# Fewer TensorE products ahead of the first MLP layer: Newton on -F and -E, paired landmarks, and batch 0's later A scores moved beside batch 1's

## The chip, the core and the metric

The kernel runs on one core of one Trainium2 chip. A core has TensorE (PE; its weight loads are listed apart as PEld), VectorE (DVE), ScalarE (ACT), GpSimd (POOL), SyncE (SP) and 16 DMA engines. Each engine works through its own list of instructions in order, and semaphores make one wait for another. The time is the device time of one execution in microseconds (us); lower is better. The kernel before took 277.86 us, the median of three runs (276.68 to 277.95).

## What is computed

Nyström attention over 8 batches of 8 heads (576 tokens, head size 64), then a two-layer MLP (512 to 2048 to 512, SiLU between) over its 4608 token rows:

```
q_lm = q.reshape(B, H, 32, 18, 64).mean(axis=3)      # 32 landmarks
k_lm = k.reshape(B, H, 32, 18, 64).mean(axis=3)
A  = softmax(q    @ k_lm^T / 8)     # 576 x 32
Bm = softmax(q_lm @ k_lm^T / 8)     # 32 x 32
C  = softmax(q_lm @ k^T    / 8)     # 32 x 576
Z  = Bm^T / (norm1(Bm) * norminf(Bm) + 1e-6)
repeat 6 times: Z = 2*Z - Z @ Bm @ Z
x  = A @ Z @ C @ v                  # heads side by side: 4608 x 512
out = silu(x @ w_in) @ w_out        # silu(h) = h * sigmoid(h)
```

## The kernel before

The eight batches go through the core one after another. For each batch there is an attention part, which makes two small things: AT, the normalised A scores transposed (line 630), and mb (lines 646 and 666), which is Z C v folded into w_in, so that the first layer is one product of mb and AT. The layer loop (line 831 on) runs 16 steps s for each batch b. A step makes 256 rows of the hidden layer (l1, line 680), runs SiLU on ACT (line 700), and adds products of the second layer of earlier tokens (l2_mm, 708; cnt says how many). The attention part of batch b+1 is woven into the steps of batch b, so that TensorE has both. The order is written out by hand: what stands in the code is the order of each engine's list.

Only batch 0 has no layers to be woven into; its attention part is the straight stretch of lines 738 to 826. Fillers (idle, line 120: products of zeros that no one reads) keep TensorE busy between its steps. DMA loads are issued by POOL, from lines 115 to 144 and from load_w_in and load_w_out calls within the stretch; POOL does some arithmetic too, in the same list.

One batch's attention part goes like this, in the names of the code. The numbers after j are the pieces of q and k: 1 and 0 are k and q of heads 0 to 3, 3 and 2 those of heads 4 to 7.

- transpose_qk (182): q and k transposed on DVE, 32x32 blocks.
- landmarks_pe (189): the sum over the 18 tokens of a landmark, as 18 products with the identity; landmarks_out (196) scales it on ACT; lm_t (254) transposes it on DVE; bd_expand (260) lays it out block-diagonally for the A scores.
- b_scores, b_max, b_exp, b_norm (268 to 315): Bm.
- c_scores, c_max, c_exp (417 to 446): C, with a transpose on TensorE and a copy (c_transpose, c_out); w_mm (476) multiplies by v, w_out (487) scales to W.
- a_scores(i), a_max(i), a_shift(i), a_exp(i), a_norm(i) for three parts i of the 576 tokens (538 to 608): A. a_shift takes the maximum off by a product on TensorE; a_norm is a_sum and a_rec on DVE and a_mul on POOL. a_transpose and a_out (611 to 630) make AT.
- z_mm, z_out, m_unit(f) or m_pair(f): mb, in four quarters f.

Between b_norm and z_mm stands the Newton iteration, in the coordinates F = Bm^T Bm / c and E = Bm / c (c is the product of the norms). Each round makes new F and E by one product with F. For batches 0 and 1 ("tiled") the state that is held is I - F, beside -E: the square of I - F is the new I - F, so for that half a copy out of PSUM is the whole step, but the E half needs E added, which ns_mm (366) does by eight more products with the identity:

```
365	
366	        def ns_mm(self, last=False):
...
379	            if self.tiled:
380	                for g in range(2):
381	                    for h in range(4):
382	                        p = slice(32 * h, 32 * h + 32)
383	                        mm(self.p[p, g, w:], ident[p, p], self.fx[p, g, w:],
384	                           start=False, stop=True)
```

ns_step (386) is the copy, on DVE or ACT by the call. Each mm() (line 77) is a weight load and a matmul on TensorE.

PSUM has eight banks, in four pools: psh (two buffers of two banks: c scores, c transposes of batch 0, atp, hps), pso (two banks: idle, batch 0's later A scores, mp, ops), psn (one: lmp, bb) and psa (one: batch 0's first A scores, wp, mp). A buffer's next user waits until the last reader of the one before is done. In before, some fillers of batch 0 write into the spare half of the c-transpose buffer (spare_bank, 228).

Of the kernel before, what the change touches and what calls it, by code (L numbers as in the profile page):

```python
# [9 lines left out]
BF = mybir.dt.bfloat16  # L10
AF = mybir.ActivationFunctionType
OP = mybir.AluOpType
AX = mybir.AxisListType


# [26 lines left out]
def kernel(  # L42
# [131 lines left out]
    nc.vector.tensor_copy(out=ident, in_=ident_f)  # L174

    eye = constp.tile([128, L], BF, tag="eye", name="eye")
    with nc.allow_low_precision(reason="zeros and ones"):
        nc.vector.tensor_reduce(out=eye, in_=ident_f.rearrange("p (h l) -> p l h", l=L),
                                op=OP.add, axis=AX.X)

# [44 lines left out]
    SPLIT = [256] + [HF] * (B - 1)  # L225
    zeros_in = []

    def spare_bank(x):
        zeros_in[:] = [x[:, 1, :]]
        return x  # L230

    class Att:
# [122 lines left out]
        def f_out(self):  # L355
            w = self.fw
            self.p = self.bb[:, 0:2 * (w + L)].rearrange("p (g n) -> p g n", g=2)
            if self.tiled:
                for g in range(2):
                    nc.vector.scalar_tensor_tensor(  # L360
                        out=self.fx[:, g, 0:w], in0=self.f0[:, g, :], scalar=self.nrm[:, g:g + 1],
                        in1=eye, op0=OP.mult, op1=OP.add)
                return
            nc.vector.tensor_tensor(out=self.fx[:, :, 0:w], in0=self.f0,  # L364
                                    in1=self.nrm.unsqueeze(2).to_broadcast((128, 2, w)),
                                    op=OP.mult)

        def ns_mm(self, last=False):
            w = self.fw
            lo = w if last else 0  # L370
            for g in range(2):
                if self.tiled:
                    for h in range(4):
                        p = slice(32 * h, 32 * h + 32)
                        mm(self.p[p, g, lo:], self.fx[p, g, 0:w], self.fx[p, g, lo:],
                           start=(g == 0), stop=False)
                else:
                    mm(self.p[:, g, lo:], self.fx[:, g, 0:w], self.fx[:, g, lo:],
                       start=(g == 0), stop=True)
            if self.tiled:  # L380
                for g in range(2):
                    for h in range(4):
                        p = slice(32 * h, 32 * h + 32)
                        mm(self.p[p, g, w:], ident[p, p], self.fx[p, g, w:],
                           start=False, stop=True)

        def ns_step(self, copy=nc.vector.tensor_copy):
            w = self.fw
            n = nsp.tile([128, 2, w + L], BF, tag=f"fx{w}", name="fx", bufs=3)
            if self.tiled:  # L390
                copy(out=n, in_=self.p)  # L391
            else:
                nc.vector.scalar_tensor_tensor(  # L393
                    out=n, in0=self.fx, scalar=2.0, in1=self.p, op0=OP.mult, op1=OP.subtract)
            self.fx = n


        def x_out(self):
            w = self.fw
            if self.tiled:  # L400
                self.x = nsp.tile([128, 2, L], BF, tag="x", name="x")
                nc.vector.tensor_scalar(out=self.x, in0=self.p[:, :, w:], scalar1=-1.0,
                                        scalar2=None, op0=OP.mult)
                return
# [47 lines left out]
        def c_transpose(self, g):  # L452
            if not self.by_dma:
                self.t[g] = (pso1("ctp", BF) if self.b else
                             spare_bank(ps2("ctp"))[:, 0, :].bitcast(BF))
# [20 lines left out]
        def w_mm(self):  # L476
            vv = self.v.rearrange("p h (c d) -> p h c d", d=Dh)
            self.w = psa1("wp")[:, 0:2 * Dh].rearrange("p (g d) -> p g d", d=Dh)
            for g in range(2):
# [7 lines left out]
        def w_out(self):  # L487
            self.W = attp.tile([128, 2, Dh], BF, tag="W", name="W", bufs=1)
            for g in range(2):
                if g == 0 and self.b == 0:  # L490
                    nc.vector.tensor_scalar(out=self.W[:, g, :], in0=self.w[:, g, :],
                                            scalar1=self.wsc[:, g:g + 1], scalar2=None,
                                            op0=OP.mult)
                    continue
                nc.scalar.activation(out=self.W[:, g, :], in_=self.w[:, g, :], func=AF.Copy,
# [21 lines left out]
        def z_out(self):  # L517
            self.zwT = attp.tile([128, 4, L], BF, tag="zwT", name="zwT")
            if self.tiled:
                for k, copy in enumerate((nc.vector.tensor_copy, nc.scalar.copy)):  # L520
                    copy(out=self.zwT[:, k::2, :],
                         in_=self.zt[k].rearrange("p (g l) -> p g l", l=L))
            else:
# [108 lines left out]

        def m_unit(self, f, *copy, parts=1):
            self.m_done = f + 1
# [8 lines left out]
            for c0 in range(0, 512, 512 // parts):  # L643
                for r in range(2):
                    c = slice(c0, c0 + 512 // parts)
# [92 lines left out]
    wt = pso1("idle")  # L738
    idle(wt, 9, 512)
    lp = psn1("lmp")  # L740
    landmarks_pe(0, lp, 1, 1)
    transpose_qk(0, 1)
    landmarks_out(0, lp, 1, 1)
    idle(wt, 8)
    landmarks_pe(0, lp, 0, 1)
    transpose_qk(0, 0)
    landmarks_out(0, lp, 0, 1)
    idle(wt, 10)
    a = Att(0)
# [4 lines left out]
    landmarks_out(0, lp, 3, 1)  # L754
    idle(wt, 4)
    landmarks_pe(0, lp, 2, 1)
    transpose_qk(0, 2)
    landmarks_out(0, lp, 2, 1)
    idle(wt, 11)
    a.lm_t(1)  # L760
# [7 lines left out]
    a.a_scores(0)  # L768
    a.a_scores(2)
    a.a_scores(1)  # L770
    a.c_max(0)
# [5 lines left out]
    a.c_transpose(0)  # L777
    idle(zeros_in[0], 8)
    a.c_out(0, nc.scalar.copy)
    a.ns_mm()  # L780
    a.c_max(1)
    idle(zeros_in[0], 4)
    a.ns_step(nc.scalar.copy)
    a.c_exp(1)
    a.ns_mm()
    a.ns_step()
    a.a_max(0)
    idle(zeros_in[0], 4)
    a.ns_mm()
    a.ns_step(nc.scalar.copy)  # L790
    a.c_transpose(1)
    a.ns_mm()
    a.c_out(1, nc.scalar.copy)
    a.a_shift(0)
    a.a_exp(0)
    a.ns_step()
    a.w_scale()
    a.a_max(1)
    load_w_out(0)
    load_w_out(1)  # L800
# [24 lines left out]
    landmarks_pe(1, lp0[:, 0, :], 0, 1, (9, 18))  # L825
    landmarks_out(1, lp0[:, 0, :], 0, 2)

# [3 lines left out]
    for b in range(B):  # L831
# [14 lines left out]
        for s in range(NDC):  # L846
# [3 lines left out]
            if s <= d and b < 2:  # L850
                l1(s)
                act(s)
                if s == 0:
                    lp = psn1("lmp")
                if b == 1:
                    landmarks_pe(2, lp, ORD[s], 1)
# [40 lines left out]
            elif s == d + 2:  # L897
                n = cnt[s]
                a.a_start()
                a.a_scores(0)  # L900
                a.a_scores(1)
                a.c_max(1)
                a.a_max(0)
                a.a_max(1)
                a.c_exp(0)
                a.c_exp(1)
                if b:
                    l2_mm(min(n - 4, 6))
# [175 lines left out]
```

## Time and profile before

| what | us |
|---|---|
| median of three runs | 277.86 |
| the profiled execution, whole | 278.91 |
| its span, first to last instruction | 277.2 |
| TensorE busy, matmuls | 259.0 (93%) |
| ACT busy | 178.2 (64%) |
| DVE busy | 151.9 (55%) |
| POOL busy | 117.7 (42%) |
| TensorE busy in the first 60 us | 49.64 |
| first product of layer 1 starts | 27.14 |
| first SiLU starts | 28.18 |
| f_mm of batch 1 (start of its Newton iteration) | 40.88 |

Times in the profile count from the first instruction. A line of the timeline has start, duration, engine, line, operation and shape, and in brackets the engine's idle time before it and what ended that. "issue" is idle time for which the profile shows no cause. The page's 40 slices are 6.93 us each; a digit is a tenth. PEclk is the clock granted to TensorE, of full speed; in the window view it is the first number behind the engines' columns. DMA share is the mean busy share of the 16 DMA engines, and may go over 1.00 where transfers overlap.

Where the batch-0 stretch and the first layer steps stand: k and q of batch 0 land at 5.54, 6.96, 9.10 and 10.48 us; w_mm runs from 19.82 to 23.19; the layer loop starts at 27.14; batch 1's scores start at 33.91, and its exponentials need the Exp table on ACT (34.63 to 36.12) and then the Silu table again (41.48 to 42.98).

### The profile page before, as it was taken

How to read it: one execution, taken by the hardware profiler on the slowest of the kernel's cores; microseconds unless marked ns; L12 is line 12 of the kernel's file. 1: busy time of each engine (PE TensorE's matmuls, PEld its weight loads, DVE VectorE, ACT ScalarE, POOL GpSimd, SP SyncE). 2: the span in 40 equal slices, each digit the busy share in tenths (PEclk: the TensorE clock that was granted, in tenths of full speed). 3: DMA queues.
4: the chain of work that ended last, by engine and by line, in shares of the span. 5: the costliest groups of instructions: out<-in, count | busy, mean ns of one | idle time of the engine just before them, and what ended most of it. 6: DMA issues, size and time to landing. Idle time of an engine off the chain costs nothing.

```text
span 277.2 us, 7127 instructions
## 1 busy us (share of the span) xinstructions
PE 259.0 (93%) x2920; PEld 149.8 (54%) x2958; DVE 151.9 (55%) x379; ACT 178.2 (64%) x341; POOL 117.7 (42%) x169
## 2 busy tenths in 40 slices
PE   7876879999999999999999999999999999999994
PEld 3654645557565456555655555455645565555541
DVE  5764578264769565838684856836784653100000
ACT  2354686686946985669766965788578846646511
POOL 8434044611598439751895179333971030100000
PEclk9997779999999999999999999999999999999999
DMA  6999999392888791919656955605091312110111
GB/s 107 194 211 207 206 206 169 72 201 65 144 175 135 136 190 48 156 43 197 106 77 133 191 135 78 145 38 97 14 187 47 95 50 71 40 76 38 40 76 76
DMA packets 37792, 32.38 MB, mean 117 GB/s; under 512 B 18816, under 2 KB 29056, under 8 KB 37760
## 3 DMA queue, kind: packets, MB, share of 16 engines
q0 software_dynamic: 15104, 18.35, 41.2%
q1 hardware_dynamic: 22656, 13.57, 18.8%
q8 instruction: 23, 0.38, 0.5%
q14 instruction: 9, 0.07, 0.1%
HBM read 36.70 MB, written 9.44 MB: 166 GB/s over the span
## 4 chain that ended last, share of the span: by engine, by line
PE 81%; issue 6%; ACT 5%; DMA 3%; POOL 3%; DVE 1%; ACTq 0%; POOLq 0%; DVEq 0%
PE ops L78 43%; PE hps L78 21%; PE bb L78 4%; PE sa L78 4%; DMA nat<-in_q_dram 3%; PE scp L78 2%; PE mp L78 2%; PE wp L78 2%; PE lmp L78 1%; PE mpp L78 1%; ACT ex L575 1%; ACT L152 1%; ACT eCT L462 1%; ACT ost L726 1%; POOL an L601 1%
## 5 line engine op out<-in xcount | busy, mean ns | idle before, releaser
L78 PE MATMUL ops<-w_out_sb,gT 128*128 128x512 bf16 x538 | 141.3, 379 | 3.4 <-issue 2.2
L700 ACT ACTIVATE gT<-hps 128x576 bf16<-128x576 f32 (+2 forms) x128 | 82.5, 650 | 56.6 <-PE hps L78 56.4
L78 PE MATMUL hps<-AT,mb 128*128 128x288 bf16 (+2 forms) x512 | 82.9, 287 | 1.3 <-ACT gT L700 0.7
L78 PEld LDWEIGHTS <-gT 128*128 128x128 bf16 x576 | 52.8, 98 | 47.3 <-issue 5.6
L78 PEld LDWEIGHTS <-mb 128*128 128x128 bf16 x512 | 48.8, 98 | 27.1 <-issue 1.8
L186 DVE STREAM_TRANSPOSE qkT<-nat 128x576 f32<-128x576 f32 x32 | 39.3, 1246 | 2.2 <-DMA nat<-in_k_dram 1.8
L726 ACT COPY ost<-ops 128x512 f32<-128x512 f32 x36 | 21.1, 586 | 16.0 <-PE ops L78 15.2
L601 POOL TENSOR_TENSOR an<-ex,arec 128x512 bf16<-128x512 bf16 (+1 forms) x24 | 21.1, 901 | 21.1 <-DVE arec L591 6.2
L393 DVE SCALAR_TENSOR_TENSOR fx<-fx,bb 128x320 bf16<-128x320 bf16 x30 | 14.6, 488 | 18.3 <-PE bb L78 17.8
L666 DVE CAST mb<-mp 128x512 bf16<-128x512 f32 x28 | 18.0, 685 | 11.5 <-PE mp L78 11.5
L212 POOL TENSOR_TENSOR lma<-nat 128x1152 f32<-128x1152 bf16 x10 | 23.7, 2370 | 0.0
L263 POOL COPY bd<-lmc 32x128 bf16<-32x128 bf16 (+1 forms) x32 | 8.9, 279 | 29.0 <-DVE lmc L255 28.0
L152 ACT ACT_TABLE_LOAD x16 | 20.5, 1283 | 1.1 <-PEq L1068 0.8
L986 POOL CAST gate<-fx 128x2 f32<-128x2 bf16 x6 | 1.1, 185 | 44.5 <-DVE fx L364 44.5
L78 PEld LDWEIGHTS <-ident 128*128 128x128 bf16 (+1 forms) x336 | 12.9, 103 | 8.9 <-issue 5.2
L78 PEld LDWEIGHTS <-fx 32*32 32x32 bf16 (+1 forms) x168 | 8.5, 93 | 10.5 <-DVE fx L391 0.6
L667 ACT CAST mb<-mpp 128x1024 bf16<-128x1024 f32 x14 | 14.2, 1011 | 0.0
L586 DVE TENSOR_REDUCE arec<-ex 128x16 f32<-128x512 bf16 (+1 forms) x24 | 14.0, 584 | 0.0
L78 PE MATMUL bb<-fx 32*32 32x64 bf16 (+2 forms) x168 | 13.1, 204 | 0.3 <-DVE fx L391 0.2
L78 PEld LDWEIGHTS <-qkT 128*128 128x128 bf16 (+1 forms) x160 | 10.0, 102 | 5.5 <-issue 2.7
L432 DVE TENSOR_REDUCE cmx<-scp 128x1 f32<-128x576 f32 x16 | 11.9, 753 | 1.1 <-PE scp L78 0.8
L704 POOL COPY gT<-gT 128x1024 bf16<-128x1024 bf16 x4 | 4.1, 1036 | 17.8 <-ACT gT L700 17.7
(108 smaller groups left out, 278.2 us busy)
## 6 DMA issues: line engine op xcount, KB each, us to landing
out_dram<-ost SPq DMA_DIRECT2D x36, 256.0 KB, 2.2
nat<-in_k_dram POOLq DMA_DIRECT2D x16, 288.0 KB, 6.3
nat<-in_q_dram POOLq DMA_DIRECT2D x16, 288.0 KB, 7.6
v<-in_v_dram POOLq DMA_DIRECT2D x8, 576.0 KB, 6.8
w_in_sb<-in_moe_w_in_dram POOLq DMA_DIRECT2D x4, 512.0 KB, 15.8
w_out_sb<-in_moe_w_out_dram POOLq DMA_DIRECT2D x4, 512.0 KB, 14.5
AT<-an SPq DMA_TRANSPOSE x30, 3.9
eCT<-eC SPq DMA_TRANSPOSE x12, 5.2
```

Source lines behind the costliest of these rows:

```text
L78: nc.tensor.matmul(out=o, lhsT=lhsT, rhs=rhs, start=start, stop=stop, skip_group_check=True)
L152: nc.scalar.activation(out=spare[:, 1:2], in_=spare[:, 0:1], func=func)
L186: nc.vector.transpose(out=o.rearrange("p (l t) -> p t l", t=SEG), in_=nat_t[b][:, j, :].bitcast(FP).rearrange("p (t l) -> p t l", l=L))
L212: nc.gpsimd.tensor_tensor(out=a1, in0=nat[:, :, 0:3 * w], in1=nat[:, :, 3 * w:6 * w], op=OP.add)
L393: nc.vector.scalar_tensor_tensor(out=n, in0=self.fx, scalar=2.0, in1=self.p, op0=OP.mult, op1=OP.subtract)
L432: nc.vector.tensor_reduce(out=mx, in_=self.s[g][:, :, 0:HF], op=OP.max, axis=AX.XY, negate=True)
L586: nc.vector.tensor_reduce(out=r, in_=x, op=OP.add, axis=AX.X)
L601: nc.gpsimd.tensor_tensor(out=self.an[0:pr, c:c + n, :].rearrange("p c (h l) -> p (c h) l", l=L), in0=x, in1=r.unsqueeze(2).to_broadcast(( ...
L666: nc.vector.tensor_copy(out=o[:, r, 0:512], in_=m[r])
L667: nc.scalar.copy(out=o[:, :, 512:1024], in_=m2)
L700: nc.scalar.activation(out=gT_t[b][:, 2 * s:2 * s + 2, o + c0:o + c1], in_=h[:, :, 0:c1 - c0], func=AF.Silu)
L726: nc.scalar.copy(out=ost, in_=st["ps"])
```

## The change

Newton: for batches 0 and 1 the state becomes -F beside -E. Then the step is 2 x state + product, for both halves, as one scalar_tensor_tensor on DVE (ns_step), and the identity products go. In one round of batch 0 the doubled state is added on TensorE instead, by products with a new constant ident2 = 2 I (whole=True), and the step is a copy on ACT. x_out becomes a scalar_tensor_tensor too. The constant eye goes.

Landmarks: pieces 1 and 0 of batch 0 are summed by one pass of 18 products of 128 columns instead of two of 64; for batch 1 both pairs are.

A scores: of batch 0, only part 0 stays ahead of the layers. Parts 1 and 2 move to step 5 of the layer loop, together with those of batch 1. The first part's norm is split up and moved ahead of w_out's loads. w_mm of batch 0 writes to the pso pool.

Order: fillers become fewer and wider (512 columns, all in the bank wt); the Silu table is loaded behind w_out instead of z_out; load_w_out(3) moves from the layer loop into the stretch; m_unit(0)'s copies are on DVE and ACT, with a_transpose, a_out and 12 landmark products between the two halves; m_unit(2) moves from step 1 to step 3.

```diff
-    eye = constp.tile([128, L], BF, tag="eye", name="eye")
...
+    ident2 = constp.tile([128, 128], BF, tag="ident2", name="ident2")
+    nc.vector.tensor_scalar(out=ident2, in0=ident_f, scalar1=2.0, scalar2=None, op0=OP.mult)
...
         def f_out(self):
-            if self.tiled:
-                for g in range(2):
-                    nc.vector.scalar_tensor_tensor(
-                        out=self.fx[:, g, 0:w], in0=self.f0[:, g, :], scalar=self.nrm[:, g:g + 1],
-                        in1=eye, op0=OP.mult, op1=OP.add)
-                return
...
-        def ns_mm(self, last=False):
+        def ns_mm(self, last=False, whole=False):
...
-            if self.tiled:
+            if whole:
                 for g in range(2):
                     for h in range(4):
-                        mm(self.p[p, g, w:], ident[p, p], self.fx[p, g, w:],
+                        mm(self.p[p, g, lo:], ident2[p, p], self.fx[p, g, lo:],
                            start=False, stop=True)
...
-            if self.tiled:
-                copy(out=n, in_=self.p)
+            if whole:
+                whole(out=n, in_=self.p)
             else:
                 nc.vector.scalar_tensor_tensor(
-                    out=n, in0=self.fx, scalar=2.0, in1=self.p, op0=OP.mult, op1=OP.subtract)
+                    out=n, in0=self.fx, scalar=2.0, in1=self.p, op0=OP.mult,
+                    op1=OP.add if self.tiled else OP.subtract)
...
-            self.w = psa1("wp")[:, 0:2 * Dh].rearrange("p (g d) -> p g d", d=Dh)
+            self.w = (psa1 if self.b else pso1)("wp")[:, 0:2 * Dh].rearrange("p (g d) -> p g d", d=Dh)
...
-    idle(wt, 9, 512)
+    idle(wt, 12, 512)
     lp = psn1("lmp")
-    landmarks_pe(0, lp, 1, 1)
     transpose_qk(0, 1)
-    landmarks_out(0, lp, 1, 1)
-    idle(wt, 8)
-    landmarks_pe(0, lp, 0, 1)
+    landmarks_pe(0, lp, 0, 2)
     transpose_qk(0, 0)
-    landmarks_out(0, lp, 0, 1)
-    idle(wt, 10)
+    landmarks_out(0, lp, 0, 2)
+    idle(wt, 3, 512)
...
     a.a_scores(0)
-    a.a_scores(2)
-    a.a_scores(1)
+    idle(wt, 2, 512)
     a.c_max(0)
     a.c_exp(0)
     a.b_norm()
     a.f_mm()
     a.b_scale()
     a.f_out()
     a.c_transpose(0)
-    idle(zeros_in[0], 8)
+    idle(wt, 2, 512)
     a.c_out(0, nc.scalar.copy)
     a.ns_mm()
     a.c_max(1)
-    idle(zeros_in[0], 4)
+    idle(wt, 2, 512)
+    a.ns_step()
+    a.c_exp(1)
+    a.ns_mm(whole=True)
+    a.a_max(0)
     a.ns_step(nc.scalar.copy)
-    a.c_exp(1)
-    a.ns_mm()
-    a.ns_step()
-    a.a_max(0)
-    idle(zeros_in[0], 4)
-    a.ns_mm()
-    a.ns_step(nc.scalar.copy)
+    idle(wt, 1, 512)
     a.c_transpose(1)
+    a.a_shift(0)
+    a.a_exp(0)
     a.ns_mm()
     a.c_out(1, nc.scalar.copy)
-    a.a_shift(0)
-    a.a_exp(0)
+    a.ns_step()
+    a.a_sum(0)
+    idle(wt, 1, 512)
+    a.ns_mm()
+    idle(wt, 2, 512)
     a.ns_step()
     a.w_scale()
-    a.a_max(1)
+    a.a_rec(0)
+    a.a_mul(0)
     load_w_out(0)
     load_w_out(1)
-    lp0 = ps2("lmp")
-    landmarks_pe(1, lp0[:, 0, :], 1, 1, (0, 9))
+    a.w_mm()
     a.ns_mm()
+    a.w_out()
+    table(AF.Silu)
     a.ns_step()
-    a.a_max(2)
-    a.w_mm()
+    idle(wt, 1, 512)
     a.ns_mm(last=True)
-    a.w_out()
     a.x_out()
-    a.a_norm(0)
     load_w_out(2)
-    a.a_shift(1)
-    a.a_exp(1)
-    a.a_shift(2)
-    a.a_exp(2)
+    load_w_out(3)
     at = ps2("atp")
     a.z_mm(at[:, 1, :])
     a.z_out()
-    table(AF.Silu)
-    landmarks_pe(1, lp0[:, 0, :], 1, 1, (9, 18))
-    landmarks_pe(1, lp0[:, 0, :], 0, 1, (0, 9))
-    a.m_unit(0, nc.vector.tensor_copy, nc.vector.tensor_copy, parts=2)
-    a.a_transpose(0, at[:, 0, :].bitcast(BF))
-    a.a_out(nc.scalar.copy)
-    landmarks_pe(1, lp0[:, 0, :], 0, 1, (9, 18))
-    landmarks_out(1, lp0[:, 0, :], 0, 2)
+    lp = psn1("lmp")
+    landmarks_pe(1, lp, 0, 2, (0, 6))
+
+    def first_tokens():
+        a.a_transpose(0, at[:, 0, :].bitcast(BF))
+        a.a_out(nc.vector.tensor_copy)
+        landmarks_pe(1, lp, 0, 2, (6, SEG))
+
+    a.m_unit(0, nc.vector.tensor_copy, nc.scalar.copy, parts=2, between=first_tokens)
...
-                elif s < 2:
-                    a0.m_unit(s + 1, nc.scalar.copy, nc.scalar.copy if s == 0 else
-                              nc.vector.tensor_copy)
-                    landmarks_pe(1, lp, ORD[2 + s], 1)
-                    idle(lp[:, 256:512], 6)
+                elif s == 0:
+                    landmarks_out(1, lp, 0, 2)
+                    a0.m_unit(1, nc.scalar.copy, nc.scalar.copy)
+                elif s == 1:
+                    idle(lp[:, 256:512], 8, 256)
+                elif s == 2:
+                    landmarks_pe(1, lp, 2, 2)
+                    landmarks_out(1, lp, 2, 2)
+                else:
+                    idle(lp[:, 256:512], 4, 256)
                 if b == 0:
                     transpose_qk(1, ORD[s])
                     if s == 0:
-                        load_w_out(3)
                         load_v(1)
                         a = Att(1)
+                    elif s == 1:
                         a.lm_t(0)
-                    elif s == 1:
-                        landmarks_out(1, lp, 2, 2)
                     elif s == 3:
                         a.lm_t(1)
                         a.bd_expand(0, 2, nc.gpsimd.tensor_copy)
+                        a0.m_unit(2, nc.vector.tensor_copy, nc.scalar.copy)
...
             elif s == d + 2:
                 a.a_start()
...
+                if b == 0:
+                    a0.a_scores(1)
+                    a0.a_scores(2)
+                    a.a_scores(0)
+                    a.c_max(1)
+                    for i in (1, 2):
+                        a0.a_max(i)
+                    a.a_max(0)
+                    a.c_exp(0)
+                    a.c_exp(1)
+                    for i in (1, 2):
+                        a0.a_shift(i)
+                        a0.a_exp(i)
+                    a.a_scores(1)
+                    a.a_max(1)
```

More of the change, by code (lines that the diff above doesn't have):

```diff
@@ L174 @@
     nc.vector.tensor_copy(out=ident, in_=ident_f)
-    eye = constp.tile([128, L], BF, tag="eye", name="eye")
-    with nc.allow_low_precision(reason="zeros and ones"):
-        nc.vector.tensor_reduce(out=eye, in_=ident_f.rearrange("p (h l) -> p l h", l=L),
-                                op=OP.add, axis=AX.X)
+    ident2 = constp.tile([128, 128], BF, tag="ident2", name="ident2")
+    nc.vector.tensor_scalar(out=ident2, in0=ident_f, scalar1=2.0, scalar2=None, op0=OP.mult)
     def transpose_qk(b, j):
@@ L225 @@
     SPLIT = [256] + [HF] * (B - 1)
[L226 to L230, printed above, removed]
     class Att:
@@ L375, in ns_mm @@
                         mm(self.p[p, g, lo:], self.fx[p, g, 0:w], self.fx[p, g, lo:],
-                           start=(g == 0), stop=False)
+                           start=(g == 0), stop=not whole)
                 else:
@@ L383, in ns_mm, with ns_step @@
                         p = slice(32 * h, 32 * h + 32)
-                        mm(self.p[p, g, w:], ident[p, p], self.fx[p, g, w:],
+                        mm(self.p[p, g, lo:], ident2[p, p], self.fx[p, g, lo:],
                            start=False, stop=True)
-        def ns_step(self, copy=nc.vector.tensor_copy):
+        def ns_step(self, whole=None):
             w = self.fw
             n = nsp.tile([128, 2, w + L], BF, tag=f"fx{w}", name="fx", bufs=3)
-            if self.tiled:
-                copy(out=n, in_=self.p)
+            if whole:
+                whole(out=n, in_=self.p)
             else:
                 nc.vector.scalar_tensor_tensor(
-                    out=n, in0=self.fx, scalar=2.0, in1=self.p, op0=OP.mult, op1=OP.subtract)
+                    out=n, in0=self.fx, scalar=2.0, in1=self.p, op0=OP.mult,
+                    op1=OP.add if self.tiled else OP.subtract)
             self.fx = n
@@ L401, in x_out @@
                 self.x = nsp.tile([128, 2, L], BF, tag="x", name="x")
-                nc.vector.tensor_scalar(out=self.x, in0=self.p[:, :, w:], scalar1=-1.0,
-                                        scalar2=None, op0=OP.mult)
+                nc.vector.scalar_tensor_tensor(
+                    out=self.x, in0=self.fx[:, :, w:], scalar=-2.0, in1=self.p[:, :, w:],
+                    op0=OP.mult, op1=OP.subtract)
                 return
@@ L454, in c_transpose @@
                 self.t[g] = (pso1("ctp", BF) if self.b else
-                             spare_bank(ps2("ctp"))[:, 0, :].bitcast(BF))
+                             ps2("ctp")[:, 0, :].bitcast(BF))
                 for c in range(VC):
@@ L489, in w_out @@
             for g in range(2):
[L490 to L494, printed above, removed]
                 nc.scalar.activation(out=self.W[:, g, :], in_=self.w[:, g, :], func=AF.Copy,
@@ L519, in z_out @@
             if self.tiled:
-                for k, copy in enumerate((nc.vector.tensor_copy, nc.scalar.copy)):
-                    copy(out=self.zwT[:, k::2, :],
-                         in_=self.zt[k].rearrange("p (g l) -> p g l", l=L))
+                for k in range(2):
+                    nc.vector.tensor_copy(out=self.zwT[:, k::2, :],
+                                          in_=self.zt[k].rearrange("p (g l) -> p g l", l=L))
             else:
@@ L630, in a_out, with m_unit @@
             copy(out=self.AT[:, :, self.ar[0]:self.ar[1]], in_=self.at)
-        def m_unit(self, f, *copy, parts=1):
+        def m_unit(self, f, *copy, parts=1, between=None):
             self.m_done = f + 1
@@ L643, in m_unit @@
             for c0 in range(0, 512, 512 // parts):
+                if c0 and between:
+                    between()
                 for r in range(2):
@@ L754 @@
     landmarks_out(0, lp, 3, 1)
-    idle(wt, 4)
+    idle(wt, 2, 512)
     landmarks_pe(0, lp, 2, 1)
@@ L758 @@
     landmarks_out(0, lp, 2, 1)
-    idle(wt, 11)
+    idle(wt, 3, 512)
     a.lm_t(1)
@@ L781 @@
     a.c_max(1)
-    idle(zeros_in[0], 4)
-    a.ns_step(nc.scalar.copy)
-    a.c_exp(1)
-    a.ns_mm()
-    a.ns_step()
-    a.a_max(0)
-    idle(zeros_in[0], 4)
-    a.ns_mm()
-    a.ns_step(nc.scalar.copy)
+    idle(wt, 2, 512)
[3 more added lines that the diff above has]
+    a.a_max(0)
+    a.ns_step(nc.scalar.copy)
+    idle(wt, 1, 512)
     a.c_transpose(1)
+    a.a_shift(0)
+    a.a_exp(0)
     a.ns_mm()
     a.c_out(1, nc.scalar.copy)
-    a.a_shift(0)
-    a.a_exp(0)
+    a.ns_step()
+    a.a_sum(0)
+    idle(wt, 1, 512)
+    a.ns_mm()
+    idle(wt, 2, 512)
     a.ns_step()
     a.w_scale()
-    a.a_max(1)
+    a.a_rec(0)
+    a.a_mul(0)
     load_w_out(0)
     load_w_out(1)
-    lp0 = ps2("lmp")
-    landmarks_pe(1, lp0[:, 0, :], 1, 1, (0, 9))
+    a.w_mm()
     a.ns_mm()
+    a.w_out()
+    table(AF.Silu)
     a.ns_step()
-    a.a_max(2)
-    a.w_mm()
+    idle(wt, 1, 512)
     a.ns_mm(last=True)
-    a.w_out()
     a.x_out()
-    a.a_norm(0)
     load_w_out(2)
-    a.a_shift(1)
-    a.a_exp(1)
-    a.a_shift(2)
-    a.a_exp(2)
+    load_w_out(3)
     at = ps2("atp")
@@ L852 @@
                 act(s)
-                if s == 0:
-                    lp = psn1("lmp")
                 if b == 1:
+                    if s == 0:
+                        lp = psn1("lmp")
                     landmarks_pe(2, lp, ORD[s], 1)
-                elif s < 2:
-                    a0.m_unit(s + 1, nc.scalar.copy, nc.scalar.copy if s == 0 else
-                              nc.vector.tensor_copy)
-                    landmarks_pe(1, lp, ORD[2 + s], 1)
-                    idle(lp[:, 256:512], 6)
+                elif s == 0:
[8 more added lines that the diff above has]
+                    idle(lp[:, 256:512], 4, 256)
                 if b == 0:
@@ L899 @@
                 a.a_start()
[L900 to L907, printed above, removed]
+                if b == 0:
[13 more added lines that the diff above has]
+                    a.a_max(1)
+                else:
+                    a.a_scores(0)
+                    a.a_scores(1)
+                    a.c_max(1)
+                    a.a_max(0)
+                    a.a_max(1)
+                    a.c_exp(0)
+                    a.c_exp(1)
                     l2_mm(min(n - 4, 6))
```

## The prediction

> **What bounds the kernel now.** I read the page's slices first, then the chain of work that ended last, then the busy time in windows of 3.4 us, then the timeline of the stretch they point at. From about 60 us on TensorE is busy all the time, so a microsecond won ahead of that moves everything behind it. The losses are in the first 43 us.
>
> ```profile
> span 277.2 us, 7127 instructions
> PE 259.0 (93%) x2920; PEld 149.8 (54%) x2958; DVE 151.9 (55%) x379; ACT 178.2 (64%) x341; POOL 117.7 (42%) x169
> ...
> PE   7876879999999999999999999999999999999994
> ...
> PEclk9997779999999999999999999999999999999999
> ...
> q8 instruction: 23, 0.38, 0.5%
> ```
>
> TensorE's row is full after slice 7, and the clock is low only in slices 4 to 6. Queue q8 moved 23 packets of 0.38 MB / 23 = 16.4 KB, and TensorE has 2920 + 2958 = 5878 recorded instructions: 256 to a packet. I read q8 as TensorE's own code.
>
> ```profile
> 18.48 0.79 ACT eCT L462
> 19.27 0.51 ACT ex L575
> 19.82 0.51 PE wp L78 x43
> 20.33 2.64 issue
> 22.97 0.24 PE wp L78 x5
> ```
>
> This is the chain. In the middle of w_mm, after 43 of its 48 products, TensorE stops for 2.64 us with nothing to wait for that the profile shows. Counted through the code, w_mm's 43rd is matmul 351, so 702 instructions with the weight loads; 768 = 3 x 256 is reached if some 66 unrecorded ones (preamble, waits) stand among them. The q8 packets begin at 14.42, 20.48, 26.56 and 33.37 us. Matmul 226 (instruction 512 by that count) ran at 16.9 us, 3.6 us ahead of the second packet; work resumed at 22.97, 3.6 us ahead of the third. So entering a block seems to ask for the next one: 3.6 us to the packet, 2.5 us from there to running, 6.1 us in all beside a DMA share that is full.
>
> ```profile
> 6.60:10.02 3.42, 2.54 (x60) 2.22 (x57) 2.43 (x4) 1.56 (x7) 1.90 (x4) 1.00 1.09 187
> ...
> 20.26:23.67 3.41, 0.77 (x32) 0.40 (x22) 0.44 (x4) 0.11 (x1) 0.00 (x0) 1.00 1.13 209
> 23.67:27.08 3.41, 3.27 (x49) 2.37 (x49) 2.04 (x8) 3.10 (x8) 2.33 (x3) 0.50 1.24 210
> 27.08:30.50 3.42, 3.37 (x38) 2.33 (x38) 1.53 (x3) 1.91 (x6) 1.00 (x2) 0.50 1.24 203
> 33.91:37.32 3.41, 1.43 (x58) 1.07 (x58) 2.79 (x6) 2.88 (x8) 1.67 (x6) 1.00 1.24 205
> 37.32:40.74 3.42, 3.42 (x26) 1.56 (x24) 2.60 (x7) 2.58 (x7) 1.58 (x3) 0.50 1.28 205
> ```
>
> The columns are the window, its length, the busy us of PE, PEld, DVE, ACT and POOL, the clock and the DMA. The stretch with the stop has 0.77 us of TensorE work, and the two after it run at clock 0.50. A second thin stretch (1.43) is followed by another half-speed one; one with 2.54 is not.
>
> **The change, part by part.** I lay the new order against the old rows.
>
> *Up to w_mm.* ident2 for eye (0.36) on DVE lies beside the wait for the first load. Nothing before 13.1 us moves: the four q and k pieces land at 5.54, 6.96, 9.10 and 10.48 and set the pace, the 12 wide fillers end near 6.4, and the doubled landmark pass (18 matmuls for 36) ends near 8.0, with 1.1 us to spare before the third piece. After c_scores only 8 of the 20 A-score matmuls stay, so f_mm starts near 14.15 instead of 14.53. f_out is one DVE operation of about 0.22 us for two of 0.40 together: 15.45 for 15.54. c_max(1) (0.75) now stands before the first Newton step on DVE: step at 16.1 to 16.4, where ACT's copy ended at 16.66. A step by scalar_tensor_tensor I price as the copy, 0.29: the 128x320 one takes 0.488, and 192 elements at 1.04 ns (512 against 128 wide copies: 0.69 and 0.29) fewer leave 0.29. The second step (ACT, behind c_exp(1)) ends at 17.3, for 17.64. c_transpose(1) and a_shift(0) end at 17.9, a_exp(0) 18.5, and c_out(1), behind it on ACT, at 19.3, as before (19.27). a_sum(0) (0.68) now waits for a_exp(0) on DVE, and the fourth step stands behind it: 19.2 to 19.5. w_mm has a bank of its own, so its first half starts near 19.0 and the second at 19.33, against 19.82.
>
> *The stop.* Ahead of w_mm's end I count 249 matmuls for 356. By the same 64 unrecorded ones, instruction 512 falls at matmul 224, in w_mm itself, and 256 at matmul 96, in c_scores near 12.0 us. The block asked for at 12.0 is there by 18.1; it is wanted at 19.1. The one asked for at 19.2 is there by 25.3; instruction 768 is matmul 352, in l1(3), near 27.2. So the 2.64 us go, with 1 and 2 us in hand, and with them the half clock after 23.67. [...]
>
> *To the first layer.* Fifth product 19.65, W on ACT 20.3, the Silu table (1.28 + 0.20) 21.8 and now hidden; last product 20.3 to 20.5, x 20.8, z 21.0, zwT by two DVE copies 21.4; 6 landmark matmuls wait for the first of them, then m_unit(0) ends at 22.05; a_out, between the halves on DVE, 22.9; 12 landmark matmuls until 23.0. l1(0) starts at 22.95 (was 27.14). POOL: a_mul(0) now stands ahead of load_w_out, which issues near 21 instead of 17.02. The queue covers that: w_in(3), issued at 13.78, lands only at 29.93. Without that cover w_out(0) would land 4 us later, still ahead of its use at about 37.7.
>
> *Layer steps 0 to 4 of batch 0.* ACT: act(0) 24.1, landmarks_out 24.45, two copies 25.55, act(1) 26.15, act(2) 26.75. TensorE: the paired landmarks (18 of 128 wide, about 1 us; last k and q landed at 24.90) end at 27.2, l1(3) 27.65, 4 fillers 28.1, m_unit(2) 28.5, its copies 29.2. l1(4) waits for these: 29.25, for 33.38. Won there: 4.1. DVE's four transposes at a 1.1 pitch are done by 28 and lie beside it.
>
> *The Exp stretch of batch 1.* act(4) ends 30.4, Exp table 31.9 (no longer hidden by a wait for landmarks), two b_exp 32.5, two c_exp 34.2, batch 0's two A exponentials (0.60 + 0.37, new here) 35.15. Both pso banks hold batch 0's scores, so a_scores(1) starts at 34.8; with a_scores(2) and the shift, a_exp(0) starts at 36.25 and the three end at 37.8; the m_unit(3) copy 38.4, the Silu table 39.9. act(5) starts at 39.9, for 42.89: 3.0 won, the stretch being 1.1 longer than before. The moved maxima (0.68 + 0.40 on DVE) lie beside the table and the c_exps.
>
> *Batch 1's Newton steps.* The identity products are gone: 8 in each of 6 rounds. Chain rows give 16 small products 0.21 us, so at most 6 x 0.105 = 0.6; at least nothing, where DVE (busy 1.84 of 2.00 us at 44 to 46) sets the step. I take 0.4, nearer the upper end because TensorE is busy 1.93 of those 2.00.
>
> Sum: 3.0 + 0.4 = 3.4 us. Against the profiled execution (278.91, 1.7 around its span) 275.5; it stands 1.05 above the median of the runs, so against that median 277.86 - 3.4 = 274.5.
>
> **Rivals.**
>
> *The clock drops in the Exp stretch.* From 33.6 to 34.8 TensorE waits for a bank; I count some 2.3 us of work in the 3.41 from 33.9. That is between 1.43 (dropped) and 2.54 (held). A half-speed stretch behind it costs about 1.1: m_unit 0.63 for 0.41, four second-layer products 0.35 more, the scores 0.2, the shifts 0.3, by before's rows. 275.6. [...]
>
> *The stop only moves, and the kernel is slower.* If the block asked for at 12.0 comes later than 19.1, w_mm stops again. It decides from about 9 us of delivery instead of 6.1: then 2 us or more of stop, half clock behind it (the 4.1 won up to l1(4) gone), and the Exp stretch still 1.1 longer, less 0.4: 278.5 or so. For it: all of the DMA is full there. Against it: three packets with the same 3.6 us.
>
> *The gain is covered later.* Data could set batch 1's pace: v(1) lands at 43.01, w_out(3) at 40.10, and the queue is full until 46. Against it: w_mm of batch 1 ran at 50.1 and would run near 46.7; the last quarter of w_out is wanted after 43. If a load did hold, 276.5 to 277.9.
>
> **How the numbers follow.** Forecast 0.55 (its own range 273.4 to 275.3: a Newton share of 0 to 0.6, and half a microsecond either way in the new chain), clock drop 0.25, cover 0.10, moved stop 0.10. This kernel's measurement tells about 0.5% (1.4 us) from no change, so faster is below 276.5: all of the forecast and most of the clock drop, 0.75. Same takes 0.05 of the clock drop, the cover and a little of the moved stop: 0.16. Slower: 0.09. The range runs from 272.6, if chains that I lined up in sequence overlap, to 277.4, which leaves out the moved stop and part of the cover.
>
> **What would show it.** Right: no issue gap over 0.5 us in w_mm; second q8 packet before 17 us, third near 23; clock 1.0 from 23 to 33; l1(0) at 23, l1(4) at 29.3, act(5) at 39.9. A stop in w_mm or in l1(1) to l1(3) with a packet inside it would show the moved stop; clock 0.5 behind a window of about 2.3 us of work the clock drop. I am wrong if act(5) is as early as said and the end is not.

## The result, and the profile after

The changed kernel takes 275.0 us, the median of five runs (274.94 to 275.52), beside 277.86 for before (five runs, 276.68 to 278.50): 0.991 of its time, with a 95% interval of 0.988 to 0.994. It is 2.9 us faster; 3.4 were forecast, and the forecast of 274.5 is 0.5 us off. The two profiled executions stand further apart, 277.2 and 273.3 us of span. Why, the experiments show.

The page of the changed kernel, in the lines shown of before:

```profile
span 273.3 us, 6831 instructions
...
PE 260.6 (95%) x2789; PEld 145.2 (53%) x2789; DVE 151.5 (55%) x378; ACT 177.8 (65%) x340; POOL 117.9 (43%) x169
...
PE   6989699999999999999999999999999999999994
...
PEclk9999999999999999999999999999999999999999
...
q8 instruction: 22, 0.36, 0.5%
```

The clock row is full, and 5578 TensorE instructions (2 x 2789) go with 22 packets of q8 for 23 before: 254 to a packet. Among the first slices the fifth (27.3 to 34.2 us) is thin; from the sixth on TensorE is full.

The chain of the changed kernel where before stood still:

```profile
18.28 0.24 PE bb L77 x8
18.52 0.54 PE idle L77 x2
19.06 0.49 PE wp L77 x48
19.54 0.20 PE bb L77 x8
```

All 48 products of w_mm run in one piece, and from there to the first layer TensorE's longest gap is 0.33 us, one DVE operation. Where the first two code packets lie fits the count in the prediction: they begin at 15.25 and 22.50 us, 3.3 us behind 12.0 and 3.3 behind 19.2, the two moments at which blocks were said to be asked for. The third, at 28.90, comes only 2.0 us behind matmul 352 (26.86), so the delay is not the same for every packet.

Up to w_mm's first product the changed kernel issues 201 matmuls, before 308. Of the 107 fewer, 32 are identity products of the Newton steps, 28 fillers, 27 landmark products (18 by the pairing, 9 of batch 1 moved behind w_mm), 12 A scores, and 8 products with F of a round that now follows w_mm.

TensorE's work in windows of the changed kernel, cut where before's half-speed stretches were (window, its length, busy us of PE, PEld, DVE, ACT and POOL, clock, DMA):

```profile
20.26:23.67 3.41, 2.77 (x58) 2.11 (x50) 2.14 (x7) 2.14 (x5) 3.37 (x5) 1.00 1.13 208
23.67:27.08 3.41, 3.38 (x46) 2.79 (x39) 3.41 (x5) 2.91 (x9) 0.79 (x1) 1.00 1.24 206
27.08:30.50 3.42, 2.26 (x47) 1.11 (x52) 1.58 (x4) 2.14 (x6) 2.35 (x7) 1.00 1.25 208
30.50:33.91 3.41, 2.65 (x50) 1.68 (x41) 2.89 (x5) 3.40 (x11) 0.90 (x2) 1.00 1.23 206
33.91:37.32 3.41, 2.51 (x32) 1.35 (x32) 2.12 (x7) 2.28 (x6) 0.00 (x0) 1.00 1.24 206
```

The window that held 0.77 us of TensorE work holds 2.77, and no half-speed stretch follows it.

The lead of the changed profile over the old one, mark by mark (SiLU n counts the activations of line 700 from 0):

| mark | before | after | lead | forecast lead |
|---|---|---|---|---|
| l1(0) starts | 27.14 | 22.92 | 4.22 | 4.19 |
| l1(4) starts | 33.38 | 29.08 | 4.30 | 4.13 |
| act(5) starts | 42.89 | 38.93 | 3.96 | 3.0 |
| SiLU 12 | 55.91 | 51.81 | 4.10 | 3.4 |
| SiLU 25 | 79.83 | 75.73 | 4.10 | 3.4 |
| SiLU 26 | 81.99 | 78.14 | 3.85 | 3.4 |
| span | 277.2 | 273.3 | 3.9 | 3.4 |

Up to l1(4) the forecast chain holds to 0.2 us. In the Exp stretch and behind it the sizes differ, and a quarter of a microsecond is lost at one place near 76 us.

### The profile page after: what moved, and what is told of

Its sections match the earlier page's. It is cut to its first block, busy times and chain, and to the rows that moved or that the text cites. A ratio compares the mean times of both kernels' runs of the same rounds, so it can differ in the third digit from the quotient of the medians.

```text
span 273.3 us, 6831 instructions
## 1 busy us (share of the span) xinstructions
PE 260.6 (95%) x2789; PEld 145.2 (53%) x2789; DVE 151.5 (55%) x378; ACT 177.8 (65%) x340; POOL 117.9 (43%) x169
## 4 chain that ended last, share of the span: by engine, by line
PE 82%; ACT 7%; DMA 6%; DVE 2%; issue 1%; POOL 1%; ACTq 0%; DVEq 0%; POOLq 0%
PE ops L77 43%; PE hps L77 21%; PE bb L77 4%; PE sa L77 3%; DMA eCT<-eC 3%; DMA nat<-in_q_dram 3%; PE lmp L77 2%; PE mp L77 2%; ACT L151 2%; PE wp L77 1%; PE scp L77 1%; ACT eC L430 1%; PE mpp L77 1%; ACT ex L558 1%; ACT gT L685 1%
## 5 line engine op out<-in xcount | busy, mean ns | idle before, releaser
L77 PE MATMUL ops<-w_out_sb,gT 128*128 128x512 bf16 x576 | 148.2, 380 | 0.0
L379 DVE SCALAR_TENSOR_TENSOR fx<-fx,bb 128x320 bf16<-128x320 bf16 (+1 forms) x39 | 17.1, 439 | 23.1 <-PE bb L77 22.6
L77 PEld LDWEIGHTS <-ident 128*128 128x128 bf16 (+2 forms) x194 | 9.5, 98 | 9.3 <-issue 4.5
L273 DVE TENSOR_REDUCE bmx<-bb 128x2 f32<-128x64 f32 x8 | 1.7, 217 | 18.7 <-PE bb L77 18.7
```

The costliest lines, as they stand in the source:

```text
L77: nc.tensor.matmul(out=o, lhsT=lhsT, rhs=rhs, start=start, stop=stop, skip_group_check=True)
L379: nc.vector.scalar_tensor_tensor(out=n, in0=self.fx, scalar=2.0, in1=self.p, op0=OP.mult, op1=OP.add if self.tiled else OP.subtract)
```

## The experiments

The theory: TensorE stops where its next 256 instructions have not arrived; the block is asked for on entry into the one ahead, and comes late because the DMA is full. The rival: the stop belongs to w_mm (its bank, its operands), and the gain is from the bank, the fillers or the order.

### e1: before, profiled once more

No edit.

> The kernel before, profiled once more. Theory (the stop in w_mm is TensorE waiting for its next 256 instructions): a stop of 2 to 3 us after about 43 of w_mm's 48 products again, with a packet of queue q8 beginning at its start (within 0.5 us). What the clock does behind it may differ, as its windows run free of the kernel: between none and two windows at half speed before 31 us, and with it the span by up to 1.5 us; that would make the profiled 278.91 us one of the slow ones of before, and the difference of the spans (277.2 to 273.3) larger than that of the medians. Rival (the stop is a wait of w_mm that this execution happened to have): the stop is at another product, or gone.

It took 279.71 us. TensorE's timeline in it:

```profile
21.02 0.78 PE L78 MATMUL wp<-v,eCT 96*32 96x64 bf16 x43
24.32 0.27 PE L78 MATMUL wp<-v,eCT 96*32 96x64 bf16 x5 [2.52 <-issue]
```

The stop is at the same product, 2.52 us long, and a packet begins at 21.86, 0.06 us into it. The queue's line for the stop alone, 21.80 to 24.32:

```profile
q8 instruction: 1, 0.02, 2.3%
```

The clock is another matter: here 0.50 from 19.44 to 29.68 and from 36.50 to 39.92, against 23.67 to 30.49 and 37.32 to 40.73 in the first profile. The half-speed stretches are whole multiples of 3.41 us (6.82 and 3.41 in the first profile, 10.24 and 3.42 here), but lie differently against the kernel.

Over the 65 executions of before that ran beside the experiments, the time follows the mean clock of the execution; these are the clocks with nine executions or more:

| mean clock | executions | median us |
|---|---|---|
| 0.994 | 10 | 276.7 |
| 0.988 | 9 | 277.5 |
| 0.982 | 9 | 278.6 |
| 0.981 | 14 | 278.1 |
| 0.975 | 16 | 279.2 |

Before's profiled execution (278.91 us at 0.980) lies above the median of these 65, 278.2, so the spans overstate the gain against the median. Against the executions of before with the least half speed (0.994) the change wins 276.7 - 275.0 = 1.7 us; the rest up to 2.9 goes with the clock.

### e2: the changed kernel, with the old number of instructions

```diff
-    idle(wt, 2, 512)      # four such, and two of one, between a_scores(0) and w_mm
+    tiny(24)              # and tiny(12): products of 32x32 by 32
+    def tiny(n):
+        for i in range(n):
+            p = slice(32 * (i % 4), 32 * (i % 4) + 32)
+            mm(wt[p, 0:32], zero[p, 0:32], zero[p, 0:32], start=True, stop=True)
```

> The changed kernel with the ten 512-column fillers between the first A scores and w_mm replaced by 120 products of 32x32 by 32: 110 matmuls more (220 instructions), about the same or less TensorE time. Theory (code loading): instruction 512 falls where matmul 224 does, now at the end of the fillers of the first Newton round near 15.9 us instead of in w_mm; its block, asked for near 11.7, runs from 17.7, so a stop of 1 to 2 us near 16. The next block then is asked for at 17.7 and runs from 23.8; instruction 768 (matmul 352) is at the end of w_mm, near 21: a second stop of 2 to 3 us there. l1(0) starts 3.5 to 5.5 us later than in the changed kernel (22.92), the time is 3 to 6 us longer: 278 to 281. Rival (the gain came from w_mm's bank, the wider fillers as such and the new order, not from the count): no stop, l1(0) within 0.5 us of 22.92, the time within 1 us of 275.0.

281.62 us (281.37 to 282.26), 1.012 of before (1.006 to 1.019), 6.6 more than the changed kernel. Its chain:

```profile
15.48 0.14 PE idle L77 x23
15.62 1.92 issue
17.54 0.18 PE idle L77
...
20.13 0.16 PE idle L77 x13
20.29 0.65 PE wp L77 x34
20.94 2.52 issue
23.46 0.30 PE wp L77 x8
```

Two stops, behind matmuls 223 and 351 of the list: within one matmul of the 224 and 352 that were counted. 128 matmuls, 256 instructions, lie between them. The second is again in w_mm, now with a bank of its own and in the new order, so neither bank nor order removes it. l1(0) starts at 28.59, 5.7 us late. The stops are 4.4 us of the 6.6; the clock was 0.50 from 17.84 to 31.49, and I put the other 2.2 down to that. All other parts of the change are still in this kernel, and nothing of the lead is left: fewer instructions are shown to be what the gain in front needs.

### e3: before, with 74 instructions fewer

```diff
-    idle(wt, 8)
+    idle(wt, 2, 512)      # likewise 10 -> 2, 4 -> 1, 11 -> 3; zeros_in 8 -> 2, 4 -> 1, 4 -> 1
```

> The kernel before with its 49 narrow fillers of 128 columns replaced by 12 of 512, the same columns: 37 matmuls (74 instructions) fewer ahead of w_mm and nothing else. Theory (code loading): matmul 352 is then no product of w_mm but the last ones of batch 1's landmarks behind z_mm. The stop moves there, near 21.5 us, and ends near 24: w_mm runs through, l1(0) starts 0.5 to 1.5 us ahead of 27.14, and the time is 0.3 to 1.5 us shorter. So fewer instructions alone do not remove the stop when they are not enough. Rival (a wait that belongs to w_mm): the stop of 2.6 us stays after about 43 of w_mm's products, l1(0) within 0.3 us of 27.14.

277.12 us beside 278.22, ratio 0.9975 (0.994 to 1.001), so that a gain is not shown in the time. TensorE's timeline:

```profile
19.35 0.55 PE L78 MATMUL wp<-v,eCT 96*32 96x64 bf16 x48 [0.37 <-ACT ex L575]
...
20.80 0.35 PE L78 MATMUL lmp<-nat,ident 128*128 128x64 bf16 x6
23.24 0.51 PE L78 MATMUL lmp<-nat,ident 128*128 128x64 bf16 x12 [2.09 <-issue]
```

w_mm runs through, and the stop stands in the landmark products, behind matmul 351 once more and 2.09 us long. l1(0) starts at 25.24, 1.9 ahead of before; 0.5 to 1.5 were expected. Taking these 74 instructions out moved the stop. It is gone in the changed kernel, where 7.2 us lie between matmuls 96 and 224 and 7.7 between 224 and 352.

### e4: before, with the DMA quiet when the block is asked for

```diff
-    load_w_in(0)
-    load_qk(1, (1, 0))
-    load_w_in(1)
-    load_qk(1, (3, 2))
-    load_w_in(2)
...
+    nc.gpsimd.tensor_copy(out=gate, in_=a.fx[:, :, 0])    # behind the third Newton step
+    load_w_in(0)          # and the rest of them, load_w_in(3) too
```

> The kernel before with all weight loads and batch 1's q and k held back on POOL until the third Newton step (about 18.3 us), so that the DMA engines have nothing from 13.5 to 18.4 us. Same TensorE instructions. Theory (the block is late because its DMA stands in a full DMA): the block asked for at 16.9 us arrives fast, its q8 packet begins before 18.5 instead of 20.48, and the stop in w_mm is under 0.5 us. The rest gets slower, since the loads come up to 13 us later: l1(0) from 26 us on, the whole up to 8 us longer. Rival (a fixed time per block, or no matter of loading): packet near 20.5 and a stop of over 2 us in w_mm, as before.

283.16 us (one execution), as the loads come late. DMA activity of this run from 10 to 22 us, in 40 slices of 0.3 us, and the queue's line:

```profile
DMA  9999998200000000000002000000000000903799
...
q8 instruction: 2, 0.03, 1.2%
```

The lone 2 in the empty middle is the second code packet, at 16.52 us instead of 20.48; the first came at 12.04 instead of 14.42. With nothing else in the queues the packet began when, by the count, its block was asked for: matmuls 222 to 226, by which the count has the request, run at 16.51 to 16.77. w_mm ran without a gap, but that is no proof by itself: TensorE had stood 6.94 us ahead of it, for batch 1's k. The packet's time is the evidence, and by it nearly all of the 3.6 us is time spent behind other transfers.

### e5: the changed kernel, batch 1 on the old Newton state

```diff
+            if self.old:              # b == 1: eye in f_out, copy as step, x = -p
+                for g in range(2):
+                    for h in range(4):
+                        p = slice(32 * h, 32 * h + 32)
+                        mm(self.p[p, g, w:], ident[p, p], self.fx[p, g, w:],
+                           start=False, stop=True)
```

> The changed kernel with batch 1 alone back on the old Newton state (I - F, eight identity products a round, step by a plain copy). The prediction gave this part 0.4 us, between 0 and 0.6. The two profiles show the start of batch 1's first round 3.9 us earlier, its w_mm 4.1 us earlier and the end 3.9 us earlier, so little of it seems to reach the end. Theory now: within 0.3 us of the changed kernel (274.9 to 275.4), as DVE sets the pace of those rounds. Rival (the prediction's term): 0.4 to 0.6 us longer, 275.4 to 275.7.

274.91 us (274.75 to 274.92): no loss. But the trace shows that the part is worth something and then worth nothing: SiLU 12 starts at 52.02 against 51.81 in the changed kernel, SiLU 25 at 75.94 against 75.73, and SiLU 26 at 78.02 against 78.14. The lead of 0.21 us is eaten between 25 and 26.

### e6: batch 1's scores ahead of l1(4)

```diff
             elif s == d + 1:
-                l1(s)
-                act(s)
-                l2_mm(cnt[s])
+                if b:
+                    l1(s)
+                    act(s)
+                    l2_mm(cnt[s])
...
                         a0.a_exp(i)
+                    l1(s - 1)
...
                 table(AF.Silu)
+                if b == 0:
+                    act(s - 1)
```

> The changed kernel with batch 1's scores ahead of the l1(4) of batch 0, which moves behind the c exponentials; its SiLU goes behind the second table load. Theory (the Exp stretch is bound by ACT, whose table load waits for act(4), which waits for m_unit(2)'s copies): the Exp table load starts near 29.0 instead of 30.34, batch 1's first Newton product near 37.8 instead of 39.08, and as ACT has act(4) to do behind the second table, 0.6 to 1.2 us of it reach the end: 273.8 to 274.4. Rival (TensorE bound from 37 us on, l1(4) is only moved into a stretch that had no room, or its idle gaps lower the clock): within 0.4 us of 275.0, or slower with clock 0.50 somewhere between 30 and 44 us.

274.85 us, with 274.42 to 275.04 and one of 275.97 at clock 0.988: not told apart from the changed kernel. The Exp table load starts at 29.00 as expected, 1.3 us earlier. With act(4) behind the second table, 0.34 us of that is left by SiLU 6 (40.17 for 40.51) and at SiLU 25 (75.39). SiLU 26 is 0.25 ahead, and the same place has taken some again.

### What stands between SiLU 25 and 26: e7, e11

In the changed kernel that is w_mm of batch 2. The DMA transposes of its exponentials (eCT), in the view of the tile:

```profile
L437 SPq DMA_TRANSPOSE eCT<-eC x2: 1471/2146/2822, 66.6 to 68.2; - x2
...
  PE wp L77: 0.2, 1
...
DMA to landing us min/median/max: 7.9/8.4/8.8
```

They are issued at 66.65 and 68.17 us behind batch 4's q and k (64.83 to 66.41) and land at 75.50 and 76.10; w_mm begins at 75.63 and waits. In before they landed at 79.35 and 79.95 for a w_mm at 79.72, just in time. e7 loads batch 4's q and k later:

```diff
-                if s == (5 if b == 1 else 1) and b + 3 < B:
+                if s == (12 if b == 1 else 1) and b + 3 < B:
```

> The changed kernel with batch 4's q and k loaded in step 12 of batch 1 instead of step 5, so that they are not in the DMA queues while batch 2's C exponentials are transposed by DMA (issued at 66.65 and 68.17 us, landed at 75.50 and 76.10). Theory (a gain beyond some 3.85 us meets this transfer: in the changed kernel w_mm of batch 2 waits for it, and the lead of 4.10 us over before falls to 3.85 between steps 9 and 10 of batch 1): the two transposes land before 73, w_mm does not wait, the lead stays 4.1, and the time is 0.2 to 0.35 us shorter than that of the changed kernel in this job. Rival (the lead is lost to something else there, or the load is missed later): within 0.1 us or longer.

277.12 us (276.31 to 279.84): slower. The first half of the theory held: the transposes landed at 69.71 and 71.05, and SiLU 26 follows SiLU 25 by 2.08 us instead of 2.41. But the load now meets batch 5's, and both meet batch 3's transposes, which land at 103.71 and 104.37 instead of 98.41 and 99.08. TensorE's waits from 66 to 110 us in e7:

```profile
PE wp L77 <- DMA eCT<-eC: 1.6, 2, 1.3
```

So the same collision is moved one batch on, and priced: 1.6 us at full clock. Two more runs stood on this load:

> As e7, with batch 1 on the old Newton state (as e5). Theory (the Newton change in batch 1 is worth 0.21 us, as the SiLU of step 12 shows: 51.81 against 52.02; and it was hidden by the wait for the transposed exponentials): 0.2 us longer than e7, where with the early load there was nothing between them (274.91 against 275.0). Rival (worth nothing anyway): the same as e7 within 0.1; rival (the prediction's term): 0.4.

277.12 us, the same as e7; with executions from 276.31 to 279.84 in e7 and from 276.49 to 279.18 here, 0.2 us can't be seen, and this run settles nothing. Its profile shows one source of the spread: w_mm of batch 3 waits 1.7 us for the transposes, the window from 101.60 to 105.02 holds 1.71 us of TensorE work, and the clock is 0.50 from 105.02 to 108.43.

> As e7, with batch 1's scores ahead of l1(4) (as e6). Theory: e6 was 0.34 us ahead of the changed kernel until the wait for the transposes and 0.13 behind it; without the wait 0.3 to 0.4 us less than e7, 0.5 to 0.7 less than the changed kernel: about 274.4. Rival: no less than e7 by 0.15.

278.17 us, between 275.50 and 280.31, so the median is no test of the scores either. The executions at clock 1.00 say more: three of e9 took 275.50 to 275.90, three of e7 276.33 to 277.17 and four of e8 276.49 to 277.04. By them e9 is some 1.0 us ahead; 0.6 of it is a shorter wait of w_mm for the transposes from 66 to 110 us (1.0 for 1.6 in the two profiles). (By the SiLUs e6's lead behind the wait is 0.25, not the 0.13 that stands there.)

e11 issues the load in between:

```diff
+                if s == (7 if b == 1 else 1) and b + 3 < B:
```

> The changed kernel with batch 4's q and k loaded in step 7 of batch 1 (step 5 in the changed kernel, step 12 in e7). In e7 batch 2's transposed exponentials landed at 71 us and w_mm of batch 2 did not wait, but the late load ran into batch 5's, and both into batch 3's transposes, for which w_mm of batch 3 then waited 1.6 us. Theory: issued near 71 us, behind batch 2's transposes, the load lands by 78 and meets neither: between SiLU 25 and 26 of the list (steps 9 and 10 of batch 1) 2.1 us as in e7 instead of 2.4, no wait of w_mm over 0.1 us anywhere behind, and 0.2 to 0.35 us less than the changed kernel's undisturbed 275.0: 274.65 to 274.8. Rival: a wait at another transfer, 275.0 or more.

274.87 us, four of six from 274.66 to 274.93, the others 276.12 (at clock 1.00, for which nothing here shows a cause) and 276.26 (at 0.994). The tile's view of eCT there, and TensorE's waits from 66 to 110 us:

```profile
L437 SPq DMA_TRANSPOSE eCT<-eC x2: 1288/1296/1305, 66.6 to 68.0; - x2
...
DMA to landing us min/median/max: 2.9/2.9/2.9
```

```profile
PE hps L77 <- ACT mb L652: 0.3, 1, 0.3
```

The transposes take 2.9 us instead of 8.4, no w_mm waits, and SiLU 26 comes at 77.80 for 78.14. That is shown. Of the 0.34 us, 0.15 is lost again by SiLU 40 (106.13 for 106.32); the median is 0.13 below 275.0, less than the 0.2 expected and too little for these runs to tell from nothing.

### e12: e6 and e11 together

> As e11, with batch 1's scores ahead of l1(4) (as e6). Theory: the 0.34 us of e6 now reach the end: 274.3 to 274.5 where the clock stays at 1.00. Rival: within 0.1 us of e11.

274.38 us (274.27 to 275.14), 0.987 of before (0.985 to 0.990): within the forecast, the fastest of all, 0.6 us below the changed kernel and 0.5 below e11. Five of the six lie at 274.46 or less, under every execution of the changed kernel (274.73 at the lowest).

### e10: the changed kernel again

> The changed kernel beside the three above, on the same chip: 274.9 to 275.5, clock 0.99 to 1.00 in all its executions, while those of before spread over 2 us and more with clocks from 0.975 to 0.994.

Half right. Three executions took 274.73 to 275.07, but two took 276.14 and 276.30, at clock 0.994, and one of the two was profiled:

```profile
32.69:36.10 3.41, 2.13 (x20) 1.12 (x18) 2.36 (x6) 2.28 (x8) 0.53 (x1) 1.00 1.24 208
36.10:39.51 3.41, 3.12 (x21) 1.05 (x22) 2.53 (x11) 3.19 (x5) 0.00 (x0) 0.50 1.25 205
```

This is the rival of the prediction, the clock drop in the Exp stretch, and TensorE's longest gap in the window ahead of it was 0.67 us. The two executions cost 276.2 - 275.0 = 1.2 us; the price given was 1.1. A third at clock 0.994, 275.52 in the first five, cost 0.5.

## Why the prediction was right

*The stop.* The count was right to a matmul. e1, e2 and e3 put the stop at matmul 351 of three different lists, in two places of the program, and e2 adds one at 223. The step "the 2.64 us go" is confirmed, and so is its reason. In this stretch, with the DMA full, the step from one block to the next cost 1.9 to 2.6 us in four profiles (2.64 in before's, 2.52 in e1, 1.92 and 2.52 in e2, 2.09 in e3). At matmul 224 of the changed kernel, whose block by the count had been asked for 7.2 us earlier, it cost nothing. In the list of what would show it, the packets were numbered one too high: those meant as the second (before 17) and third (near 23) are the first and second, at 15.25 and 22.50.

*The chain to the first layer and steps 0 to 4.* l1(0) at 22.95 forecast and 22.92 measured, l1(4) at 29.25 and 29.08. The cover named for load_w_out held: issued from 20.59, the first lands at 32.60, for 32.47 before.

*The Exp stretch.* This term was mis-sized. From l1(4) to act(5) 10.65 us were forecast and 9.85 measured, so the stretch grew by 0.34 us over before's 9.51, not by 1.1. I had added up ACT's rows end to end, accumulator reads included; in the changed kernel they run into one another:

```profile
32.27 0.74 ACT L430 ACTIVATE eC<-scp,cmx 128x576 bf16<-128x576 f32 x1
32.90 0.20 ACT L430 ACTIVATION_READ_ACCUMULATOR eC<-scp,cmx 128x1 f32 x1
32.99 0.74 ACT L430 ACTIVATE eC<-scp,cmx 128x576 bf16<-128x576 f32 x1
33.61 0.21 ACT L430 ACTIVATION_READ_ACCUMULATOR eC<-scp,cmx 128x1 f32 x1
33.70 0.85 ACT L558 ACTIVATE ex<-sa 128x512 bf16<-128x512 f32 x2
```

The two c exponentials were to end at 34.2, and the next one started at 33.70; a_exp(0) was to start at 36.25 and started at 35.69, the second Silu table at 38.4 and 37.52.

*Batch 1's Newton steps.* Forecast 0.4. They won 0.21 us by SiLU 12 (e5 against the changed kernel) and nothing by the end.

*The median.* The sum was made against the profiled execution and carried over to the median unchanged. That was the weak step: before's time follows its mean clock (276.7 us at 0.994, 279.2 at 0.975), and by that the part of the gain that is clock is smaller in a median execution than in the profiled one, an estimate. Against the profile the change won 3.9, against the median 2.9; 3.4 lay between by the luck of two errors, the Exp stretch the one way and the clock the other.

*The rivals.* The clock drop was given 0.25: three of the ten executions of the changed kernel ran at clock 0.994 (275.52, 276.14, 276.30), none of them a median one. The one that was profiled had its drop in the Exp stretch; where the other two had theirs is not shown. Cover by a later transfer, 0.10, was partly right, by a transfer I had not named: batch 2's eCT takes the last 0.25 us. The moved stop did not come in the changed kernel; e2 shows that it would have made it slower than before. What was held against it, that every packet takes 3.6 us, is true of before's profile alone, where the first three packets began 3.6 to 3.7 us behind matmuls 96, 224 and 352; in the changed kernel's they began 3.3, 3.3 and 2.0 us behind them.

## What to carry to other kernels

A gap on TensorE with no cause in the profile, at the head of a program whose DMA is full, is worth a count of instructions: here such gaps stood behind matmuls 223 and 351 whatever the program did there, 256 instructions apart, with a code packet beginning 0.15 us behind the gap's start in before's profile and 0.06 in e1's; with the DMA empty (e4) that packet came at 16.52 us instead of 20.48, so I take it that the code was late. Fewer, wider instructions with more time between the blocks cured it here (201 matmuls ahead of w_mm for 308; 7.2 us between matmuls 96 and 224 for 5.9); 74 instructions fewer only moved it (e3). Here the gain in front of a full TensorE lasted until the next transfer that had been just in time: of a lead of 4.10 us at SiLU 25, 3.85 were left at SiLU 26, behind transposes that in before landed at 79.35 and 79.95 for a w_mm at 79.72. Look for a transfer whose landing and first use lie closer together than the gain.

## What was not expected of the hardware

The half-speed stretches came in pieces of 3.41 us, and their phase differed between executions: they start at 23.67 and 37.32 us in before's first profile, at 19.44 and 36.50 in e1's, 0.82 us apart once whole pieces are taken off. TensorE's busy time in a full-speed piece did not by itself tell what followed. Of the pieces measured here, cut where the clock was, one with 2.21 us of TensorE work (31.98 to 35.40 in the changed kernel's profile) was followed by full speed, and ones with 2.13 (e10), 2.08 (e12, 30.62 to 34.03) and 1.95 (e1, 16.03 to 19.44) by half speed. But one with 2.32 (e4, 15.66 to 19.07) was also followed by half speed, and ones with 2.00 (e7, 102.79 to 106.21) and with 1.96 and 1.86 (e4, 32.73 to 36.14 and 39.55 to 42.97) by full speed. What decides there, these runs don't tell. The same stretch of the program, the Exp stretch, ran at clock 1.00 in one profile of the changed kernel (275.0 us) and partly at 0.50 in another (e10, 36.10 to 39.51; 276.30 us). That spreads the times by more than e5, e6 and e11 move the median, 0.09 to 0.15 us.

A DMA transpose of 128 by 768 elements took 2.9 us from issue to landing with no load beside it (e11), 7.9 and 8.8 behind one batch's q and k loads, and 10.4 and 11.1 behind two batches' (e7). Where the DMA was full, the first three code packets began 3.6 to 3.7 us (before) and 2.0 to 3.3 us (the changed kernel) behind the matmuls by which the count has them asked for; where it was empty, the second one of e4 began at 16.52, within 0.3 us of its matmuls (16.51 to 16.77).
